# Attention with a Fourier mixing layer on one core: scores and S^T read their 512 moving columns from two halves of the tile in turn

## The chip, the cores and the metric

One core of a Trainium2 chip. The metric is the device time of one execution in microseconds. The kernel before took 2922.96 us, the median of three runs (2922.64 to 2923.09).

## The reference

Two independent branches, whose outputs stand side by side in the last dimension. S is 2048, D is 1024, all in float32.

```python
# branch A: attention with 32 heads of 32 columns
qkv = (x @ wqkv).reshape(B, S, 3, H, Dh) -> q, k, v per head
scores = einsum("bhqd,bhkd->bhqk", q, k) * Dh ** -0.5
p = softmax(scores, axis=-1)
o = einsum("bhqk,bhkd->bhqd", p, v)
a_out = o.reshape(B, S, D) @ wo
# branch B: real part of a 2-d Fourier transform with given matrices
a = einsum("bsd,ed->bse", x, dft_hid_re)
b = einsum("bsd,ed->bse", x, dft_hid_im)
b_out = einsum("ts,bse->bte", dft_seq_re, a) - einsum("ts,bse->bte", dft_seq_im, b)
```

## The kernel before

TensorE works on tiles of 128 partitions. Dense products (q, k, v, branch B, the output projection) are built from sums and differences of blocks, so that fewer products are needed, and each operand is split into a high and a low half, so that a product takes three matmuls in the narrower float32 form (`fp32r`). All these matmuls are issued at line 414, in groups that accumulate into one PSUM tile: `pd` (pool psD, two buffers), or `psT` where the attention doesn't use it. The text calls them dense matmuls; the code calls their list `fills`.

The attention goes head by head. For head h, `QS` (`qs`) and `KS` (`ks`) hold 96 rows of q and k (three copies of 32 rows, high and low halves, so that one matmul gives the full product), 2048 columns, and two more rows: ones in `KS`, and in `QS` first zeros and later the negated row maxima in two halves. Three streams are issued for each head:

- **S, scores** (line 1853 in `scores`). For a tile of 128 queries (the stationary operand, from `QS`, or from the copy `QX`, `qx`, for the first four) and a half of the keys, two matmuls of 512 moving columns of `KS` fill a `psS` tile of 128 x 1024. VectorE takes the row maximum (line 1859), ScalarE the exponential and its sum over the row (line 1862). Only maxima and sums are kept. There are 16 x 2 x 2 = 64 such matmuls a head.
- **T, transposed scores S^T** (line 1975 in `transposed`). For each of 16 tiles t of 128 keys (stationary, `KS`) and each of four blocks j of 512 queries (moving, `QS`), one matmul fills a `psT` tile; ScalarE writes its exponential to a `pt` tile (line 1979). 64 matmuls a head. They wait for the maxima, which get into `QS` by two small DMAs (`m_d<-lt`, `qs<-m_d`).
- **V, products with V** (line 1994). After 5, 10 and 16 of the tiles t, four products for each t, one for each j, run side by side on 32 columns of the array each (`tile_position=(0, j * DH)`), with the `pt` tile as the moving operand in plain float32. They accumulate in a `pd` tile whose partition block j holds the 32 output columns of query block j. VectorE copies the first of the three results to `ot` (line 2005) and adds the other two (line 2007). Then the row sums' reciprocals (`rt`, natural order of queries) are multiplied in (line 2023, on GpSimd or VectorE) and `ot` is stored.

The order on every engine is made at build time by a small planner (class `Plan`), which steps through a model with a cost for each operation: `MM` for one dense, S or T matmul, `PV` for the four products of one t, `EVAC` for an evacuation. In the loop at the end of the kernel it picks the next work of TensorE: streams S, T and V by their readiness and a lead that S may have, and dense matmuls where none is ready or where the dense work has fallen behind its share: `nf / (FILL - RES) <= done / ATT`, with `ATT` the planned TensorE time of the attention. Dense matmuls that are left when the attention ends make the tail of the program.

Of the kernel before, what the change touches and what calls it, by code (L numbers as in the profile page):

```python
# [11 lines left out]
ALU = mybir.AluOpType  # L12
# [4 lines left out]
P = 128  # L17
S = 2048
D = 1024
H = 32  # L20
# [3 lines left out]
NB = 512  # L24
# [198 lines left out]
def kernel(  # L223
# [12 lines left out]
    nc = tc.nc  # L236
# [115 lines left out]
    ORDER = (1, 2, 5, 6, 7, 3, 4)  # L352
    OUTERS = [(0, q) for q in (1, 5, 6, 7, 3, 2, 4)] + [(1, q) for q in ORDER]
    TWO = {(1, q) for q in ORDER} | {(0, 2), (0, 4)}
    MM, PV, SWITCH, TINY = 0.2275, 0.853, 0.40, 0.17
    ES, ET = 1.235, 0.625
    MAX, EVAC, CAST, BIT = 1.22, 0.685, 0.415, 0.275
    SUB = 1.31
# [11 lines left out]
    SFIRST = 0.6  # L370
    ADD = 0.68
    FILL = 3 * (7 * 24 * 4 + sum(7 * 2 * 4 if (r, q) in TWO else 8 * 8 for r in range(2) for q in ORDER) + 7 * 8 * 8 +  7 * 8 * 3)
    ATT = H * (128 * MM + 16 * PV + 3 * SWITCH)


    zeros, ps = pre.tile([P, NB], F32, name="c", tag="c", bufs=3), psD.tile([P, NB], F32, name="pd")
# [5 lines left out]
    op = pl.op  # L382
# [184 lines left out]
        return Piece(xh, xl, mx, mine), Piece(wh, wl, mw, wmine)  # L567

    whole = lambda t: t

    def chunk(p, c):
        return p, lambda t: t[:, c, :]
# [35 lines left out]
    att_gate = []  # L608
# [1212 lines left out]
    got = {}  # L1821
# [7 lines left out]
    def scores(h):  # L1829
        ST = {}  # L1830
        sold, suse = small["st"].take()
        maxes, exps = [], []
        if h:
            xold, xuse = qx_r.take()

            def load_x():
                att()
                g, r0 = divmod(h, 4)
                nc.sync.dma_start(f(QX[0])[0 : 3 * DH], qk_d[2 * g][0][r0 * DH : r0 * DH + DH].rearrange("d i c -> (d i) c"))

            got[h, "x"] = op("SP", ISSUE, load_x, [*xold, *qk_st[2 * (h // 4)][0], *(att_gate if h == 1 else [])], [xuse], -2, 192)
        for n, (qt, c) in enumerate([(k % 4, k // 4) for k in range(8)] + [divmod(k, 2) for k in range(8, 32)]):
            old, users = psS_r.take()
            own = h > 0 and qt < 4
            box = {}

            def mm(n=n, qt=qt, c=c, box=box, own=own):
                if n == 0:
                    ST["negm"] = sm.tile([P, 2, NS], F32, name="negm", bufs=2)
                    ST["sums"] = sm.tile([P, 2, NS], F32, name="sums", bufs=2)  # L1850
                box["p"] = p = psS.tile([P, 1024], F32, name="psS")
                for i in range(2):
                    nc.tensor.matmul(  # L1853
                        p[:, i * NB : i * NB + NB], (QX[0] if own else QS[h % 2])[:, qt * P : qt * P + P],
                        KS[h % 2][:, c * 1024 + i * NB : c * 1024 + i * NB + NB], start=True, stop=True,
                    )

            def mx(qt=qt, c=c, box=box):
                nc.vector.tensor_reduce(out=ST["negm"][:, c, qt : qt + 1], in_=box["p"], axis=AX.X, op=ALU.max, negate=True)  # L1859

            def ex(qt=qt, c=c, box=box):
                nc.scalar.activation(box["p"], box["p"], AF.Exp, bias=ST["negm"][:, c, qt : qt + 1], accum_out=ST["sums"][:, c, qt : qt + 1])  # L1862

            a = op("PE", 2 * MM, mm, [*old, *([got.get((h, "x"))] if own else [got.get((h, 0, qt // 4)), got.get((h, "z"))]), got.get((h, 1, 2 * c)), got.get((h, 1, 2 * c + 1))],
                   [users, xuse] if own else [users])
            b = op("DVE", MAX, mx, [a] + (sold if n == 0 else []), [users, suse], 0)
            e = op("ACT", ES, ex, [b], [users, suse], 0)
            exp_of[a] = e
            maxes.append(b)
            exps.append(e)  # L1870
            Sops.setdefault(h, []).append(a)
            streams["S"].append((a, h, n))
            if n == 5 and h:
                sums(h - 1)

        nold, nuse = small["nm"].take()
        lold, luse = small["lh"].take()
        box = {}

        def nmin():  # L1880
            ST["nm"] = sm.tile([P, NS], F32, name="nm", bufs=2)
            nc.vector.tensor_reduce(out=ST["nm"], in_=ST["negm"].rearrange("p c n -> p n c"), axis=AX.X, op=ALU.min)

        def high():
            box["l"] = sm.tile([P, 2, NS], F32R, name="lh", bufs=2)
            nc.vector.tensor_reduce(out=box["l"][:, 0], in_=ST["negm"].rearrange("p c n -> p n c"), axis=AX.X, op=ALU.min)

        def low():
            nc.vector.tensor_tensor(out=box["l"][:, 1], in0=ST["nm"], in1=f(box["l"])[:, 0], op=ALU.subtract)
# [12 lines left out]
        mine[h] = (ST, suse, nuse, exps, moved)  # L1902
# [59 lines left out]
    def transposed(h):  # L1962
        moved = mine[h][4]
        todo = []
        po = {}
        oold, ouse = ot_r.take()
        for t in range(NS):
            for j in range(4):
                old, users = psT_r.take()
                pold, puse = pt_r.take()  # L1970
                box = {}

                def mm(t=t, j=j, box=box):
                    box["p"] = psT.tile([P, NB], F32, name="psT")
                    nc.tensor.matmul(box["p"], KS[h % 2][:, t * P : t * P + P], QS[h % 2][:, j * NB : j * NB + NB], start=True, stop=True)  # L1975

                def ex(box=box):
                    box["t"] = att_low().tile([P, NB], F32, name="pt", bufs=NPT)
                    nc.scalar.activation(box["t"], box["p"], AF.Exp)  # L1979

                a = op("PE", MM, mm, [*old, *moved, *(att_gate if h == t == j == 0 else []), *(got.get((h, w, k)) for w, k in ((0, j), (1, t // 4)))], [users])
                e = op("ACT", ET, ex, [a, *pold], [users, puse], -1, 0, pt_r)
                exp_of[a] = e
                streams["T"].append((a, h, 4 * t + j))
                Tops.setdefault(h, []).append(a)
                todo.append((t, j, box, e, puse))
            if t + 1 in ENDS:
# [14 lines left out]
                def gather_o(t0=t0):  # L2002
                    if t0 == 0:
                        po["o"] = att_low().tile([P, NB], F32, name="ot", bufs=2)
                        nc.vector.tensor_copy(po["o"], po["p"])
                    else:
                        nc.vector.tensor_tensor(out=po["o"], in0=po["o"], in1=po["p"], op=ALU.add)

                e = op("DVE", EVAC, gather_o, [v] + (oold if t0 == 0 else []), [ouse], -1)
                streams["V"].append((v, h, e))  # L2010
# [155 lines left out]
```

## Time and profile before

| | before |
|---|---|
| median of three runs | 2922.96 us |
| profiled execution, its own time | 2929.45 us |
| its span | 2927.7 us |
| mean granted clock of TensorE | 0.999 |
| matmul records: dense, line 414 | 6528 |
| scores, line 1853 | 2048 |
| S^T, line 1975 | 2048 |
| products with V, line 1994 (two for each) | 4096 |

The profile is one execution of the program. Its page gives the busy time of each engine and groups of instructions by line; a matmul's span reaches from its start to the end of its drain, so spans of consecutive matmuls overlap, and the time that one takes up is read from the distance between starts in the timeline. "PEld" are the weight loads, which run beside the matmuls. In a group, the numbers after the bar are the busy time in us, the mean span of one in ns, and the idle time of the engine ahead of them with what ended most of it.

### The profile page before, as it was taken

The numbers are of one execution on the slowest core, as the hardware profiler recorded it, in microseconds if no ns is written. First come the engines' busy times: TensorE is split into PE (matmuls) and PEld (weight loads), VectorE is DVE, ScalarE is ACT, GpSimd is POOL, SyncE is SP. The second block draws the span as 40 slices with busy tenths as digits, with TensorE's granted clock in tenths as the row PEclk, the third lists the DMA queues.
The fourth block names the chain that finished last, engine by engine and source line by source line (L and its number), as shares of the span: only waits on it lengthen the run. The fifth ranks groups of instructions, "written<-read, shape, count | busy, mean of one in ns | idle before, by whom it ended". The sixth has DMA issues, their size and how long they took to land.

```text
span 2927.7 us, 47039 instructions
## 1 busy us (share of the span) xinstructions
PE 2904.0 (99%) x14728; PEld 2107.2 (72%) x14728; DVE 2386.5 (82%) x3251; ACT 2373.3 (81%) x4509; POOL 1241.3 (42%) x975
## 2 busy tenths in 40 slices
PE   9999999999999999999999999999999999999999
PEld 8887776777667777777676677667667777777777
DVE  7679888788788887788888898888988788788745
ACT  5348898888888888988999898898889888888741
POOL 2325534142233433337655456666675352243200
PEclk9999999999999999999999999999999999999999
DMA  9989978697789988867899776887876665677558
GB/s 345 349 298 328 314 225 272 222 346 269 268 289 339 309 297 287 291 213 218 291 348 333 226 223 216 276 272 229 271 229 208 204 180 181 193 246 226 188 191 287
DMA packets 485844, 768.18 MB, mean 262 GB/s; under 512 B 120382, under 2 KB 153406, under 8 KB 485470
## 3 DMA queue, kind: packets, MB, share of 16 engines
q1 hardware_dynamic: 485452, 765.04, 79.4%
q8 instruction: 119, 1.95, 0.3%
q14 instruction: 129, 1.06, 0.1%
q10 hardware_dynamic: 144, 0.13, 0.0%
HBM read 511.74 MB, written 253.25 MB: 261 GB/s over the span
## 4 chain that ended last, share of the span: by engine, by line
PE 75%; DMA 4%; DVE 1%; ACT 1%; SPq 0%; issue 0%; POOL 0%; DVEq 0%; ACTq 0%; POOLq 0%
PE pd L414 34%; PE psT L1975 14%; PE pd L1994 13%; PE psS L1853 13%; PE psT L414 2%; ACT psS L1862 1%; DVE negm L1859 1%; DMA qs<-m_d 1%; DMA slot<-in_ct 0%; DMA g<-in_ct 0%; DMA hl<-ha_d 0%; ACT pt L1979 0%; DMA m_d<-lt 0%; DMA ha_d<-slot 0%; DMA g<-g_d 0%
## 5 line engine op out<-in xcount | busy, mean ns | idle before, releaser
L414 PE MATMUL pd<-slot,hl 128*128 128x512 f32 x5028 | 1446.7, 390 | 4.2 <-DMA hl<-ha_d 1.4
L1979 ACT ACTIVATE pt<-psT 128x512 f32<-128x512 f32 x2048 | 1191.5, 668 | 260.7 <-PE psT L1975 258.5
L1859 DVE TENSOR_REDUCE negm<-psS 128x1 f32<-128x1024 f32 x1024 | 1240.7, 1221 | 198.3 <-PE psS L1853 190.1
L1862 ACT ACTIVATE psS<-psS,negm 128x1024 f32<-128x1024 f32 x1024 | 1189.2, 1161 | 47.4 <-DVE negm L1859 44.5
L414 PEld LDWEIGHTS pd<-slot,hl 128*128 128x128 f32 x5028 | 943.6, 188 | 204.8 <-DVE negm L1859 2.7
L1975 PE MATMUL psT<-qs,ks 128*128 128x512 f32 x2048 | 802.4, 395 | 4.4 <-DMA qs<-m_d 3.2
L1975 PEld LDWEIGHTS psT<-qs,ks 128*128 128x128 f32 x2048 | 382.2, 188 | 160.0 <-issue 53.0
L1853 PE MATMUL psS<-ks,qs 128*128 128x512 f32 x1552 | 473.1, 391 | 4.2 <-ACT psS L1862 4.2
L1994 PE MATMUL pd<-pt,vt 128*32 128x512 f32 x4096 | 460.9, 596 | 1.2 <-DVE e L723 0.9
L1853 PEld LDWEIGHTS psS<-ks,qs 128*128 128x128 f32 x1552 | 289.5, 188 | 69.1 <-ACT psS L1862 11.0
L504 POOL TENSOR_TENSOR slot<-raw,slot 128x512 fp32r<-128x512 f32 x153 | 196.2, 1291 | 316.1 <-DVE slot L501 116.6
L1994 PEld LDWEIGHTS pd<-pt,vt 128*32 128x32 f32 x4096 | 123.4, 110 | 285.1 <-issue 268.3
L504 POOL TENSOR_TENSOR slot<-slot,slot 128x512 fp32r<-128x512 f32 x183 | 234.3, 1292 | 206.1 <-DVE slot L501 54.5
L1862 ACT ACTIVATION_READ_ACCUMULATOR psS<-psS,negm 128x1 f32 x1024 | 287.0, 280 | 0.0
L504 POOL TENSOR_TENSOR hl<-raw,hl 128x512 fp32r<-128x512 f32 x122 | 156.8, 1289 | 257.4 <-DVE hl L501 84.7
L479 POOL TENSOR_TENSOR raw<-raw,g 128x512 f32<-128x512 f32 x119 | 153.3, 1291 | 226.6 <-ACT pt L1979 31.3
L414 PE MATMUL pd<-slot,slot 128*128 128x512 f32 x780 | 210.6, 389 | 0.1
L414 PEld LDWEIGHTS pd<-slot,slot 128*128 128x128 f32 x780 | 146.4, 188 | 30.9 <-DVE e L723 0.4
L1853 PE MATMUL psS<-ks,qx 128*128 128x512 f32 x496 | 151.0, 394 | 3.3 <-ACT psS L1862 3.2
L479 DVE TENSOR_TENSOR raw<-raw,g 128x512 f32<-128x512 f32 x141 | 103.3, 738 | 23.6 <-DMA g<-in_ct 6.6
L1853 PEld LDWEIGHTS psS<-ks,qx 128*128 128x128 f32 x496 | 91.7, 188 | 34.6 <-issue 9.2
L479 POOL TENSOR_TENSOR slot<-slot,slot 128x512 f32<-128x512 f32 x79 | 102.1, 1302 | 27.5 <-DVE slot L479 11.3
(140 smaller groups left out, 2167.6 us busy)
## 6 DMA issues: line engine op xcount, KB each, us to landing
hl<-ha_d SPq DMA_DIRECT2D x134, 512.0 KB
slot<-in_ct SPq DMA_DIRECT2D x144, 256.0 KB
qk_d<-e SPq DMA_DIRECT2D x52, 512.0 KB
qs<-qk_d SPq DMA_DIRECT2D x128, 192.0 KB
ks<-qk_d SPq DMA_DIRECT2D x128, 192.0 KB
raw<-g_d SPq DMA_DIRECT2D x96, 256.0 KB
ha_d<-hl SPq DMA_DIRECT2D x42, 512.0 KB
raw<-in_ct SPq DMA_DIRECT2D x80, 256.0 KB
```

What stands on the lines that cost most here:

```text
L414: nc.tensor.matmul(box["ps"], a[1]((a[0].hi, a[0].lo)[u]()), b[1]((b[0].hi, b[0].lo)[v]()), start=k == 0, stop=k == n - 1)
L479: (nc.gpsimd if e == "POOL" else nc.vector).tensor_tensor(out=dest(), in0=dest() if a is None else a.get(), in1=other["q"] if "q" in other ...
L504: (nc.gpsimd if e == "POOL" else nc.vector).tensor_tensor(out=lo(), in0=raw(), in1=f(hi()), op=ALU.subtract)
L1853: nc.tensor.matmul(p[:, i * NB : i * NB + NB], (QX[0] if own else QS[h % 2])[:, qt * P : qt * P + P], KS[h % 2][:, c * 1024 + i * NB : c * ...
L1859: nc.vector.tensor_reduce(out=ST["negm"][:, c, qt : qt + 1], in_=box["p"], axis=AX.X, op=ALU.max, negate=True)
L1862: nc.scalar.activation(box["p"], box["p"], AF.Exp, bias=ST["negm"][:, c, qt : qt + 1], accum_out=ST["sums"][:, c, qt : qt + 1])
L1975: nc.tensor.matmul(box["p"], KS[h % 2][:, t * P : t * P + P], QS[h % 2][:, j * NB : j * NB + NB], start=True, stop=True)
L1979: nc.scalar.activation(box["t"], box["p"], AF.Exp)
L1994: nc.tensor.matmul(po["p"][j * DH : j * DH + DH, :], VT[h][:, k, :], box["t"], start=(k == t0), stop=(k == t), tile_position=(0, j * DH),)
```

## The change

The moving operand of each S and T matmul is read through a view that takes its 512 columns in the order 0, 256, 1, 257, and so on. In S this permutes the keys within a tile, and maxima and sums over keys don't depend on their order. In T it permutes the queries within a block of 512, so the `pt` tile and the result of the products with V have their queries in the new order; the copy and the additions that take this result out of PSUM read it with a step of two and write the two halves of `ot` one after the other, which restores the order. The planner gets a cost `MS` for these matmuls.

```diff
-    MM, PV, SWITCH, TINY = 0.2275, 0.853, 0.40, 0.17
+    MM, MS, PV, SWITCH, TINY = 0.2275, 0.2165, 0.853, 0.40, 0.17
...
-    ATT = H * (128 * MM + 16 * PV + 3 * SWITCH)
+    ATT = H * (128 * MS + 16 * PV + 3 * SWITCH)
...
+    def turns(t):
+        return t.rearrange("p (i n) -> p n i", i=2)
+    def order_of(t):
+        return t.rearrange("p (n i) -> p i n", i=2)
+    def as_two(t):
+        return t.rearrange("p (i n) -> p i n", i=2)
...
                     nc.tensor.matmul(
                         p[:, i * NB : i * NB + NB], (QX[0] if own else QS[h % 2])[:, qt * P : qt * P + P],
-                        KS[h % 2][:, c * 1024 + i * NB : c * 1024 + i * NB + NB], start=True, stop=True,
+                        turns(KS[h % 2][:, c * 1024 + i * NB : c * 1024 + i * NB + NB]), start=True, stop=True,
...
-            a = op("PE", 2 * MM, mm, [*old, ...
+            a = op("PE", 2 * MS, mm, [*old, ...
...
-                    nc.tensor.matmul(box["p"], KS[h % 2][:, t * P : t * P + P], QS[h % 2][:, j * NB : j * NB + NB], start=True, stop=True)
+                    nc.tensor.matmul(box["p"], KS[h % 2][:, t * P : t * P + P], turns(QS[h % 2][:, j * NB : j * NB + NB]), start=True, stop=True)
...
-                a = op("PE", MM, mm, [*old, *moved, ...
+                a = op("PE", MS, mm, [*old, *moved, ...
...
-                        nc.vector.tensor_copy(po["o"], po["p"])
+                        nc.vector.tensor_copy(as_two(po["o"]), order_of(po["p"]))
                     else:
-                        nc.vector.tensor_tensor(out=po["o"], in0=po["o"], in1=po["p"], op=ALU.add)
+                        nc.vector.tensor_tensor(out=as_two(po["o"]), in0=as_two(po["o"]), in1=order_of(po["p"]), op=ALU.add)
```

The lines move down by 11: scores are issued at line 1864, S^T at 1986, the products with V at 2005, and their evacuations at 2016 and 2018. Since the planner works with the new cost, the order moves too. On TensorE, in the middle of the attention (after the last products with V of the sixth head), the rhythm of before is this, with dense matmuls (line 414) between S^T and scores:

```order
L1994 MATMUL pd<-pt,vt 32x512 x24
L1975 MATMUL psT<-qs_709,ks_710 128x512 x2
L1853 MATMUL psS<-ks_2716,qx 128x512 x4
L414 MATMUL pd<-slot_5667,hl 128x512
L1975 MATMUL psT<-qs_709,ks_710 128x512
L414 MATMUL pd<-slot_6181,hl 128x512
L1975 MATMUL psT<-qs_709,ks_710 128x512
L414 MATMUL pd<-slot_6181,hl 128x512 x2
L414 MATMUL pd<-slot_6208,hl 128x512 x3
```

And at the same place of the changed kernel:

```order
L2005 MATMUL pd<-pt,vt 32x512 x24
L1986 MATMUL psT<-qs_709,ks_710 128x512 x2
L1864 MATMUL psS<-ks_2717,qx 128x512 x4
L414 MATMUL pd<-slot_4928,hl 128x512
L1986 MATMUL psT<-qs_709,ks_710 128x512
L414 MATMUL pd<-slot_4928,hl 128x512
L1986 MATMUL psT<-qs_709,ks_710 128x512
L414 MATMUL pd<-slot_4928,hl 128x512
L414 MATMUL pd<-slot_4968,hl 128x512 x3
```

The rhythm of the streams is the same; the dense matmuls between them are others, from another point of their list. On TensorE at the end of the attention, around the last products with V of the program, before:

```order
L1975 MATMUL psT<-qs_2715,ks_2716 128x512
L414 MATMUL pd<-slot_31285,hl 128x512 x2
L414 MATMUL pd<-slot_31291,hl 128x512 x3
L414 MATMUL pd<-slot_31306,hl 128x512 x3
L1994 MATMUL pd<-pt,vt 32x512 x24
L414 MATMUL pd<-slot_31314,hl 128x512 x3
L414 MATMUL psT<-slot_30483,hl 128x512 x3
```

And changed:

```order
L1986 MATMUL psT<-qs_2716,ks_2717 128x512
L414 MATMUL pd<-slot_30654,hl 128x512
L414 MATMUL pd<-slot_30915,hl 128x512 x3
L414 MATMUL pd<-slot_31189,hl 128x512 x3
L2005 MATMUL pd<-pt,vt 32x512 x24
L414 MATMUL pd<-slot_31194,hl 128x512 x3
L414 MATMUL pd<-slot_31221,hl 128x512 x3
```

From the last products with V to the end, 153 rows of dense matmuls stood before (459 matmuls) and 139 stand now (417): 42 matmuls have moved from the tail into the attention.

More of the change, by code (lines that the diff above doesn't have):

```diff
@@ L1862, in ex @@
                 nc.scalar.activation(box["p"], box["p"], AF.Exp, bias=ST["negm"][:, c, qt : qt + 1], accum_out=ST["sums"][:, c, qt : qt + 1])
-            a = op("PE", 2 * MM, mm, [*old, *([got.get((h, "x"))] if own else [got.get((h, 0, qt // 4)), got.get((h, "z"))]), got.get((h, 1, 2 * c)), got.get((h, 1, 2 * c + 1))],
+            a = op("PE", 2 * MS, mm, [*old, *([got.get((h, "x"))] if own else [got.get((h, 0, qt // 4)), got.get((h, "z"))]), got.get((h, 1, 2 * c)), got.get((h, 1, 2 * c + 1))],
                    [users, xuse] if own else [users])
@@ L1979, in ex @@
                     nc.scalar.activation(box["t"], box["p"], AF.Exp)
-                a = op("PE", MM, mm, [*old, *moved, *(att_gate if h == t == j == 0 else []), *(got.get((h, w, k)) for w, k in ((0, j), (1, t // 4)))], [users])
+                a = op("PE", MS, mm, [*old, *moved, *(att_gate if h == t == j == 0 else []), *(got.get((h, w, k)) for w, k in ((0, j), (1, t // 4)))], [users])
                 e = op("ACT", ET, ex, [a, *pold], [users, puse], -1, 0, pt_r)
```

## The prediction

> **What bounds the kernel now.** I read the head of the page first: the span, the busy time of each engine, and by slice the clock that TensorE was granted.
>
> ```profile
> span 2927.7 us, 47039 instructions
> PE 2904.0 (99%) x14728; PEld 2107.2 (72%) x14728; DVE 2386.5 (82%) x3251; ACT 2373.3 (81%) x4509; POOL 1241.3 (42%) x975
> PEclk9999999999999999999999999999999999999999
> ```
>
> TensorE (PE) has only 2927.7 - 2904.0 = 23.7 us of the span without a matmul under way, at full clock all along, and no other engine is busy for more than 82%. The second view is the list of waits, cut to TensorE:
>
> ```profile
> PE psS L1853 <- ACT psS L1862: 7.4, 9, 1.9
> PE psT L1975 <- DMA qs<-m_d: 3.2, 4, 1.7
> ...
> PE psT L1975 <- ACT pt L1979: 1.1, 2, 0.6
> ```
>
> Its longest entry is 7.4 us in nine waits. So the time is the sum of what TensorE streams, and a matmul that gets shorter or longer moves the end almost undiluted. Third come the groups of the page: how many matmuls of each kind there are, and what ScalarE (ACT) and VectorE (DVE) spend on the tiles that these fill.
>
> ```profile
> L1979 ACT ACTIVATE pt<-psT 128x512 f32<-128x512 f32 x2048 | 1191.5, 668 | 260.7 <-PE psT L1975 258.5
> L1859 DVE TENSOR_REDUCE negm<-psS 128x1 f32<-128x1024 f32 x1024 | 1240.7, 1221 | 198.3 <-PE psS L1853 190.1
> ...
> L1975 PE MATMUL psT<-qs,ks 128*128 128x512 f32 x2048 | 802.4, 395 | 4.4 <-DMA qs<-m_d 3.2
> L1975 PEld LDWEIGHTS psT<-qs,ks 128*128 128x128 f32 x2048 | 382.2, 188 | 160.0 <-issue 53.0
> L1853 PE MATMUL psS<-ks,qs 128*128 128x512 f32 x1552 | 473.1, 391 | 4.2 <-ACT psS L1862 4.2
> L1994 PE MATMUL pd<-pt,vt 128*32 128x512 f32 x4096 | 460.9, 596 | 1.2 <-DVE e L723 0.9
> ...
> L1853 PE MATMUL psS<-ks,qx 128*128 128x512 f32 x496 | 151.0, 394 | 3.3 <-ACT psS L1862 3.2
> ```
>
> The change touches 2048 + 1552 + 496 = 4096 matmuls. Their mean of 391 to 395 ns isn't what one costs, since each begins before the last one has drained. The cost is the step from start to start, which the timeline shows where no wait falls between (columns: start, us, engine, line, tile, shape, count). First one row of products with V, then a stretch of all kinds:
>
> ```profile
> 655.30 5.36 PE L1994 MATMUL pd<-pt,vt 128*32 128x512 f32 x48 [0.22 <-DVE c L671]
> ```
>
> ```profile
> 700.53 0.61 PE L1853 MATMUL psS<-ks,qs 128*128 128x512 f32 x2
> 700.98 0.39 PE L1975 MATMUL psT<-qs,ks 128*128 128x512 f32 x1
> 701.21 0.39 PE L414 MATMUL pd<-slot,hl 128*128 128x512 f32 x1
> 701.43 0.39 PE L1975 MATMUL psT<-qs,ks 128*128 128x512 f32 x1
> 701.66 1.07 PE L414 MATMUL pd<-slot,hl 128*128 128x512 f32 x4
> 702.57 0.61 PE L1853 MATMUL psS<-ks,qs 128*128 128x512 f32 x2
> ...
> 705.38 4.50 PE L1994 MATMUL pd<-pt,vt 128*32 128x512 f32 x40
> ```
>
> From 700.53 to 702.57 nine matmuls start, scores, S^T and dense ones alike: 2.04/9 = 0.2267 us each. The products with V give the measure to set beside this, here with the first and last start of all their records:
>
> ```profile
> L1994 PE MATMUL pd<-pt,vt x4096: 592/592/1061, 278.0 to 2818.0; 128*32 128x512 f32 x196
> ```
>
> Eight more of these records (48 against 40) take 5.36 - 4.50 = 0.86 us. Their outputs are 32 partitions wide, so four run side by side, each reading its own tile, and a set of four takes 0.43 us. A product leaves two records, and such a set takes nearly twice the 0.2267 us of the other matmuls; I read this as two passes over the columns in each record, 0.43/2 = 0.215 us for 512 columns. On this reading the array and PSUM can take 512 columns in 0.215 us, and a matmul that reads one run of 512 words takes 11.7 ns longer.
>
> By the Trainium skill, "TensorE: Matmul & The Clock Gate", section "Wait — 56ns, not 53.3ns?", warm matmuls of 512 columns start 215.7 ns apart. The trace agrees for the products with V and not for the matmuls of 226.7 ns; that figure as the new step would make the saving 45.1 us in place of the 47.9 below.
>
> **The change part by part.** *The moving operand in turns.* 4096 matmuls read column 0 of the first half, column 0 of the second, column 1 of the first, and so on. No row of before shows such a read. The bounds come from the products with V. At best reading stops being a limit and the step falls to 0.215 us (0.2125 if both times are rounded unluckily); at worst every word that isn't next to the last one needs an access of its own, and the matmul goes at the pace of a single stream there, 512 words in 0.43 us. I take 0.215. The 11.7 ns are the same for each of the tiles read (ks, qs, hl) and whatever DMA, ScalarE and VectorE do meanwhile, so they look like a limit of one run of words; and four streams from four tiles, which together read 4 x 512 words in 0.43 us, twice the words per time of the single run, don't show them. Two halves in turn are nearer to this case than to one stream at half pace, though two words from one port are not two streams; that is the weak point. Sum: 4096 x 0.0117 = 47.9 us off.
>
> *Weight loads.* Unchanged in number, 188 ns each, and they lie under the matmul before. 188 is still under 215, so they don't become the bound; what is left as cover falls from 39 to 27 ns.
>
> *Putting the queries right.* The 96 evacuations of the products with V (32 copies, 64 additions) read PSUM with a step of two words.
>
> ```profile
> L2007 DVE TENSOR_TENSOR ot<-ot,pd 128x512 f32<-128x512 f32 x64 | 43.9, 686 | 85.0 <-PE pd L1994 84.9
> ...
> L2005 DVE COPY ot<-pd 128x512 f32<-128x512 f32 x32 | 22.1, 690 | 26.3 <-PE pd L1994 26.2
> ```
>
> Bounds: as now, 0.69 us; or as if the skipped words were read too, 1024 columns, 1.22 us by the L1859 row. That is 0 to 96 x 0.53 = 51 us on VectorE over the 2540 us of the attention stage (278 to 2818). A gain is excluded since no word less is read. I cost it at nothing on the end: VectorE waits 85.0 + 26.3 us just ahead of these very instructions, and while they run TensorE has S^T, scores and the other accumulator bank to go on with. Behind them on VectorE stand row maxima, so without that cover it is the exponentials, and then scores, that come late, by at most those 51 us.
>
> *The order.* The planner reckons 0.2165 for these matmuls instead of 0.2275 and moves dense matmuls forward: after the last product with V there stand 139 rows of three matmuls, and there were 153. Those 14 x 3 = 42 matmuls (9.5 us) leave the tail and enter the attention stage; TensorE runs each of them once either way, so this adds nothing. Their DMA loads and the casts ahead of them move with them.
>
> *What gets late next.* The attention stage gets shorter with the same exponentials and maxima in it.
>
> Busy time in two windows of it (PE, weight loads, DVE, ACT, POOL, each with its count; then clock, DMA share and GB/s):
>
> ```profile
> 600.00:800.00 200.00, 199.20 (x1037) 140.25 (x1028) 165.89 (x225) 173.52 (x333) 66.13 (x52) 1.00 0.85 294
> ...
> 1400.00:1600.00 200.00, 199.17 (x1034) 138.82 (x1033) 177.84 (x241) 182.76 (x349) 116.61 (x92) 1.00 0.95 323
> ```
>
> ACT is busy in them for 87% and, at the fullest, 91%. The stage loses 47.9 - 9.5 = 38 of its 2540 us, 1.5%, so 87% becomes 88%, and 91% becomes 93%: tighter, not full. The waits of TensorE on ACT and on the maxima's DMA, 7.4 + 3.2 + 1.1 = 11.7 us, will grow; I give back 8 us, an estimate of two thirds more.
>
> *Sum.* The profiled execution took 2929.45 us with a span of 2927.7, 6.5 above the median of the runs, 2922.96. In its span: 2927.7 - 47.9 + 8 = 2887.8. Against the median: 2922.96 - 39.9 = **2883 us**.
>
> **Rivals.** *A word from elsewhere costs an access of its own* (the other side). Place: each of the 4096 matmuls, on TensorE itself, with nothing to hide it. Price at the full bound: (0.43 - 0.2267) x 4096 = 833 us, time 3756; with half the words held over, some 3340. It decides from a step of 0.2281 on, where 1.4 ns x 4096 passes the 5.8 us that are 0.2%. For it speaks that all reads of before are of words in a row, so nothing shows the opposite; against it, that four scattered streams at once run unhindered. I give it 0.18.
>
> The Trainium skill, "Advanced Engine Details and Errata", section "Memory Cachelines", stands on this rival's side: SBUF is read in lines of 16 bytes, two hits on a line are needed to cover the latency, and a new line at each access is penalised. In turn, every word is on another line than the one before. No run here shows it yet; if each line is held until its four words are used, the rule doesn't bite.
>
> *The 11.7 ns aren't of reading* but of, say, changing 128 weight columns per matmul where the products with V change 32. Then the change doesn't do what it says: the step stays 0.2267, VectorE has up to 51 us more, mostly covered, and the order is planned for a pace that isn't there: 2925. For it: the width of the weights differs too between the rows that I compare. 0.08.
>
> *The exponentials hold the pace.* Scores come sooner, but psS has two buffers and each is freed by ACT. If half of the gain is lost in these waits: 2899 to 2903. Against it stand ACT's 87% and 7.4 us. 0.06.
>
> **How the numbers follow.** The forecast has 0.68; its own range is 2864 (step 0.2125, nothing given back) to 2899. With the held pace and the unchanged step the range is 2862 to 2930, which leaves out 0.18 for the costly read. A measurement of this kernel can tell about 0.2%, 5.8 us, from no change: faster 0.68 + 0.06 = 0.74, same 0.08, slower 0.18.
>
> **What would show it.** The groups of the two changed lines should have a mean near 380 ns (391 to 395 less 11.7) and the timeline steps of 0.215 between them, with the dense matmuls still at 0.227; near 390 means the second rival, near 590 the first. The two evacuation lines show 0.69 to 1.22 us. TensorE's waits on ACT should stay under 20 us and ACT's share in the attention windows rise to 88%. I am wrong altogether if the step doesn't change, or grows, or if TensorE's idle time rises by more than some 25 us.

## The result, and the profile after

The changed kernel took 2902.96 us, the median of four runs (2897.03 to 2908.37), against 2923.03 us before: ratio 0.9931, 95% interval 0.9914 to 0.9948. It is faster by 20 us, half of the 40 that were forecast. Its runs are 11.4 us apart, those of before 1 us. The profiled execution was its fastest, 2897.03 us, while the one of before was 6.5 us above the median; so the two profiles are 32 us apart, and 12 of these are the scatter of single executions.

The head of the page of the changed kernel:

```profile
span 2894.9 us, 47047 instructions
PE 2868.7 (99%) x14728; PEld 2110.3 (73%) x14728; DVE 2364.3 (82%) x3249; ACT 2362.7 (82%) x4485; POOL 1268.1 (44%) x1001
```

TensorE is still the bound. Its groups, line by line:

```profile
L414 PE MATMUL pd<-slot,hl 128*128 128x512 f32 x5076 | 1487.2, 392 | 1.7 <-DVE hl L504 1.2
...
L1986 PE MATMUL psT<-qs,ks 128*128 128x512 f32 x2048 | 779.6, 384 | 1.2 <-DMA qs<-m_d 0.7
...
L1864 PE MATMUL psS<-ks,qs 128*128 128x512 f32 x1552 | 457.4, 380 | 9.7 <-ACT psS L1873 9.5
...
L1864 PE MATMUL psS<-ks,qx 128*128 128x512 f32 x496 | 144.9, 383 | 4.3 <-ACT psS L1873 3.9
...
L2018 DVE TENSOR_TENSOR ot<-ot,pd 128x512 f32<-128x512 f32 x64 | 44.0, 687 | 93.4 <-PE pd L2005 93.2
```

Scores and S^T fell from 391 to 395 ns to 380 to 384, as forecast. But the dense matmuls at line 414, which read as before, went from 390 to 392; their group before was this:

```profile
L414 PE MATMUL pd<-slot,hl 128*128 128x512 f32 x5028 | 1446.7, 390 | 4.2 <-DMA hl<-ha_d 1.4 <-DVE negm L1859 1.3 <-POOL hl L504 0.8
```

Two nanoseconds in a mean of thousands are worth a look, and the timeline shows where they are (start, us, engine, line, tile, shape, count):

```profile
1300.33 0.59 PE L1864 MATMUL psS<-ks,qx 128*128 128x512 f32 x2
1300.76 0.39 PE L414 MATMUL pd<-slot,hl 128*128 128x512 f32 x1
1300.99 0.38 PE L1986 MATMUL psT<-qs,ks 128*128 128x512 f32 x1
1301.20 0.39 PE L414 MATMUL pd<-slot,hl 128*128 128x512 f32 x1
1301.43 0.38 PE L1986 MATMUL psT<-qs,ks 128*128 128x512 f32 x1
1301.65 1.08 PE L414 MATMUL pd<-slot,hl 128*128 128x512 f32 x4
1302.57 0.59 PE L1864 MATMUL psS<-ks,qs 128*128 128x512 f32 x2
```

Two scores take 0.43 us, 0.215 each. A dense matmul behind one in turns takes 0.23 (1300.76 to 1300.99, and 1301.20 to 1301.43), where it took 0.2267 before. The waits of TensorE on the scores' buffers have grown too, from 7.4 us in 9 waits:

```profile
PE psS L1864 <- ACT psS L1873: 13.5, 25, 1.3
...
PE psT L1986 <- DMA qs<-m_d: 0.7, 2, 0.4
...
PE psT L1986 <- ACT pt L1990: 0.3, 1, 0.3
```

The trace holds the start of every matmul. Summing the distances from each start to the next by the kind of the first one shares out TensorE's whole time, waits included. In us, for the profiled executions of before, of the changed kernel, and of the experiments below. The second row is the kernel before as it ran behind the blocks of the last experiment, a second trace of it, which started with its first loads done; the column "all" is left out there. The last two columns are the mean step of a dense matmul directly behind scores or S^T, and of the second one behind (only steps up to 241 ns, so without waits):

| | dense | scores | S^T | V | with the warm-up, all | first behind, ns | second, ns |
|---|---|---|---|---|---|---|---|
| before | 1494.6 | 477.1 | 489.5 | 456.3 | 2921.0 | 227.2 | 226.9 |
| before, behind blocks | 1492.9 | 475.1 | 488.2 | 453.8 | | 227.2 | 227.0 |
| changed | 1505.1 | 453.6 | 473.9 | 452.7 | 2888.8 | 230.9 | 229.4 |
| changed, again | 1506.7 | 454.4 | 474.2 | 456.1 | 2895.1 | 231.0 | 229.4 |
| turns, old order | 1510.7 | 452.8 | 466.6 | 453.2 | 2887.0 | 231.0 | 228.9 |
| order alone | 1490.8 | 478.6 | 495.6 | 454.4 | 2923.0 | 227.0 | 226.8 |
| scores only, old order | 1510.9 | 450.3 | 497.3 | 452.7 | 2914.7 | 230.3 | 231.3 |
| all in turns, old order | 1437.6 | 465.0 | 501.9 | 454.0 | 2862.0 | 215.8 | 215.9 |
| all in turns, replanned | 1431.1 | 463.4 | 490.8 | 456.5 | 2845.4 | 215.9 | 215.8 |

From the first row to that of the changed kernel, scores and S^T lost 39.1 us. Their steps without waits went from 227.9 and 227.4 to 215.5 and 215.4 ns, about 50 us in 4096 matmuls; so some 11 us came back as longer waits. Dense matmuls gained 10.5 us. Against the second trace of before, which has fewer waits, scores and S^T lost 35.8 us, so that some 14 came back, and dense matmuls gained 12.2. The changed kernel's second profile gives 34.7, 15 and 13.8.

Two theories came out of this. *Neighbours and waits*: a matmul that reads words in a row runs slower behind one that reads in turns, whatever the order. *Order*: the planner's new order waits more, by itself. They may both hold, and the experiments take them apart.

### The profile page after: what moved, and what is told of

It reads as the page before. It is cut to its first block, busy times and chain, and to the rows that moved or that the text cites. A ratio compares the mean times of both kernels' runs of the same rounds, so it can differ in the third digit from the quotient of the medians.

```text
span 2894.9 us, 47047 instructions
## 1 busy us (share of the span) xinstructions
PE 2868.7 (99%) x14728; PEld 2110.3 (73%) x14728; DVE 2364.3 (82%) x3249; ACT 2362.7 (82%) x4485; POOL 1268.1 (44%) x1001
## 4 chain that ended last, share of the span: by engine, by line
PE 69%; DMA 2%; ACT 2%; DVE 1%; issue 0%; SPq 0%; POOL 0%; DVEq 0%; ACTq 0%; POOLq 0%
PE pd L414 33%; PE psT L1986 12%; PE pd L2005 12%; PE psS L1864 11%; PE psT L414 2%; ACT psS L1873 1%; ACT pt L1990 1%; DVE negm L1870 0%; DMA g<-in_ct 0%; DMA ks<-qk_d 0%; DMA qs<-m_d 0%; DMA hl<-ha_d 0%; DMA m_d<-lt 0%; DMA g<-so_d 0%; DMA o_d<-ot 0%
## 5 line engine op out<-in xcount | busy, mean ns | idle before, releaser
L414 PE MATMUL pd<-slot,hl 128*128 128x512 f32 x5076 | 1487.2, 392 | 1.7 <-DVE hl L504 1.2
L414 PEld LDWEIGHTS pd<-slot,hl 128*128 128x128 f32 x5076 | 953.9, 188 | 189.4 <-DVE hl L504 1.6
L1986 PE MATMUL psT<-qs,ks 128*128 128x512 f32 x2048 | 779.6, 384 | 1.2 <-DMA qs<-m_d 0.7
L1864 PE MATMUL psS<-ks,qs 128*128 128x512 f32 x1552 | 457.4, 380 | 9.7 <-ACT psS L1873 9.5
L479 POOL TENSOR_TENSOR raw<-raw,g 128x512 f32<-128x512 f32 x147 | 189.7, 1294 | 243.4 <-DMA raw<-in_xb 25.3
L504 POOL TENSOR_TENSOR hl<-raw,hl 128x512 fp32r<-128x512 f32 x111 | 142.5, 1287 | 209.7 <-DVE hl L501 42.5
L1864 PE MATMUL psS<-ks,qx 128*128 128x512 f32 x496 | 144.9, 383 | 4.3 <-ACT psS L1873 3.9
L2018 DVE TENSOR_TENSOR ot<-ot,pd 128x512 f32<-128x512 f32 x64 | 44.0, 687 | 93.4 <-PE pd L2005 93.2
L1343 POOL TENSOR_TENSOR slot<-slot 128x512 f32<-128x512 f32 x44 | 56.7, 1293 | 143.5 <-DMA slot<-in_ct 71.5
```

The lines of the kernel that those rows point to most:

```text
L414: nc.tensor.matmul(box["ps"], a[1]((a[0].hi, a[0].lo)[u]()), b[1]((b[0].hi, b[0].lo)[v]()), start=k == 0, stop=k == n - 1)
L479: (nc.gpsimd if e == "POOL" else nc.vector).tensor_tensor(out=dest(), in0=dest() if a is None else a.get(), in1=other["q"] if "q" in other ...
L504: (nc.gpsimd if e == "POOL" else nc.vector).tensor_tensor(out=lo(), in0=raw(), in1=f(hi()), op=ALU.subtract)
L1343: made = op("POOL", SUB, lambda e, part=part, kind=ALU.add if terms[1][0] > 0 else ALU.subtract: (nc.gpsimd if e == "POOL" else nc.vector) ...
L1864: nc.tensor.matmul(p[:, i * NB : i * NB + NB], (QX[0] if own else QS[h % 2])[:, qt * P : qt * P + P], turns(KS[h % 2][:, c * 1024 + i * NB ...
L2018: nc.vector.tensor_tensor(out=as_two(po["o"]), in0=as_two(po["o"]), in1=order_of(po["p"]), op=ALU.add)
```

## The experiments

**The order apart from the reads.** Two kernels: the turns with the planner's old number, so that every engine has the order of before; and the new order with the reads and evacuations of before.

```diff
-    MM, MS, PV, SWITCH, TINY = 0.2275, 0.2165, 0.853, 0.40, 0.17
+    MM, MS, PV, SWITCH, TINY = 0.2275, 0.2275, 0.853, 0.40, 0.17
```

> The reads in turns are kept, the planner gets 0.2275 for scores and S^T again, so that every engine has the order of before. Theory 'order': the 20 us that are missing against the forecast were lost by the new order, so the old order gives about 2883 to 2890. Theory 'neighbours and waits': dense matmuls behind a matmul in turns take 4 ns more (10 us in all) and TensorE waits more on ACT whatever the order, so the time is 2898 to 2908 again, and the step of a dense matmul behind scores or S^T is again near 0.231.

Measured: 2895.86 us (2891.96 to 2898.72), ratio 0.9903, interval 0.9887 to 0.9919. This lies between the two ranges, so neither theory has all of it.

```diff
-                        turns(KS[h % 2][:, c * 1024 + i * NB : c * 1024 + i * NB + NB]), start=True, stop=True,
+                        KS[h % 2][:, c * 1024 + i * NB : c * 1024 + i * NB + NB], start=True, stop=True,
...
-                    nc.tensor.matmul(box["p"], KS[h % 2][:, t * P : t * P + P], turns(QS[h % 2][:, j * NB : j * NB + NB]), start=True, stop=True)
+                    nc.tensor.matmul(box["p"], KS[h % 2][:, t * P : t * P + P], QS[h % 2][:, j * NB : j * NB + NB], start=True, stop=True)
...
-                        nc.vector.tensor_copy(as_two(po["o"]), order_of(po["p"]))
+                        nc.vector.tensor_copy(po["o"], po["p"])
                     else:
-                        nc.vector.tensor_tensor(out=as_two(po["o"]), in0=as_two(po["o"]), in1=order_of(po["p"]), op=ALU.add)
+                        nc.vector.tensor_tensor(out=po["o"], in0=po["o"], in1=po["p"], op=ALU.add)
```

> The changed order (planner at 0.2165) with the reads and the evacuations of before. Theory 'order': the new order is worse by itself, 2930 to 2945. Theory 'neighbours and waits': the order by itself is worth nothing, 2920 to 2927, and the dense matmuls are back at 0.2267 behind scores and S^T.

Measured: 2933.07 us (2926.87 to 2937.82), ratio 1.0031, interval 1.0020 to 1.0042. So the new order by itself costs 9 us against the 2923.72 of the kernel before, and with the old order the turns bring 28 us. The old order beats the changed kernel by about 7 us (5 us against its second set of runs below), but there the intervals overlap. The theory of neighbours holds as well: with the old order the dense step behind a matmul in turns is 231.0 ns, and with the new order and no turns it is 227.0. What the new order costs is seen in the table's sums for scores and S^T, 478.6 + 495.6 us against 477.1 + 489.5. Most of it stands between an S^T and the scores that follow: the steps over 241 ns there exceed the usual 227 by 17.7 us in all, against 8.9 before.

TensorE's first row of waits in the kernel with the order alone, against 7.4 us in 9 waits before:

```profile
PE psS L1864 <- ACT psS L1873: 10.4, 21, 1.1
```

**The grain of the turns.** Next, reads in pairs of neighbouring words: for the dense matmuls (with PSUM written in the same order, so that nothing has to be put right), and for scores and S^T.

```diff
-nc.tensor.matmul(box["ps"], a[1]((a[0].hi, a[0].lo)[u]()), b[1]((b[0].hi, b[0].lo)[v]()), start=k == 0, stop=k == n - 1)
+nc.tensor.matmul(pairs(box["ps"]), a[1]((a[0].hi, a[0].lo)[u]()), pairs(b[1]((b[0].hi, b[0].lo)[v]())), start=k == 0, stop=k == n - 1)
...
+    def pairs(t):
+        return t.rearrange("p (i n k) -> p n i k", i=2, k=2)
```

> As the changed kernel, and the dense matmuls too read their 512 columns from two halves, in pairs of neighbouring words (0, 1, 256, 257, ...), and write PSUM in the same order of pairs, so that each column lands at its own place. Theory 'one run': any matmul that reads one run of words is held to 0.2267 and two runs lift it, so the dense step falls to 0.2155 and the extra 4 ns go too: 6528 matmuls go from 1505 to about 1420 us, and with an order planned for slower ones 2825 to 2860. Rival: pairs on the PSUM side cost what the reads gain, or more: dense step 0.227 or above, 2900 or above.

Measured: 3568.32 us, ratio 1.2203 (1.2186 to 1.2220). Neither side of the expectation had this size.

```diff
     def turns(t):
-        return t.rearrange("p (i n) -> p n i", i=2)
+        return t.rearrange("p (i n k) -> p n i k", i=2, k=2)
...
     def order_of(t):
-        return t.rearrange("p (n i) -> p i n", i=2)
+        return t.rearrange("p (n i k) -> p i n k", i=2, k=2)
...
     def as_two(t):
-        return t.rearrange("p (i n) -> p i n", i=2)
+        return t.rearrange("p (i n k) -> p i n k", i=2, k=2)
```

> As the changed kernel, with scores and S^T reading pairs of neighbouring words from the two halves in turn (0, 1, 256, 257, ...) and the evacuation put right accordingly. Theory 'one run': two runs are enough whatever the grain, step 0.2155 and 2895 to 2908. Rival 'grain': the gain comes from each word being apart from the word before it, so pairs keep part of the 11 ns: step 0.220 to 0.2267, 2912 to 2925.

Measured: 3384.26 us, ratio 1.1572 (1.1557 to 1.1588). The groups of the kernel with pairs in scores and S^T, and below them the dense group of the kernel with dense pairs:

```profile
L1986 PE MATMUL psT<-qs,ks 128*128 128x512 f32 x2048 | 1029.0, 507 | 0.0
L1864 PE MATMUL psS<-ks,qs 128*128 128x512 f32 x1552 | 642.6, 504 | 2.4 <-ACT psS L1873 2.4
```

```profile
L414 PE MATMUL pd<-slot,hl 128*128 128x512 f32 x5076 | 2020.0, 503 | 1.1 <-DVE hl L504 1.1
```

The span of a matmul went from 384 to 507 ns and its step to 0.333 us. The dense matmuls in pairs, with PSUM written in pairs as well, have the same step (median 0.333), so the writing isn't what costs. Both theories fall: two runs in turn don't relieve the read by being two.

A third grain: one run with a step of two, so that no word follows its neighbour.

```diff
     def turns(t):
-        return t.rearrange("p (i n) -> p n i", i=2)
+        return t.rearrange("p (n i) -> p i n", i=2)
...
-                        nc.vector.tensor_copy(as_two(po["o"]), order_of(po["p"]))
+                        nc.vector.tensor_copy(order_of(po["o"]), as_two(po["p"]))
                     else:
-                        nc.vector.tensor_tensor(out=as_two(po["o"]), in0=as_two(po["o"]), in1=order_of(po["p"]), op=ALU.add)
+                        nc.vector.tensor_tensor(out=order_of(po["o"]), in0=order_of(po["o"]), in1=as_two(po["p"]), op=ALU.add)
```

> As the changed kernel (its order too), but scores and S^T read their 512 columns with a step of two: 0, 2, 4, ... and then 1, 3, 5, ...; the evacuation is put right accordingly. After the runs with pairs (step 0.333) the theory of two runs doesn't hold as it stood. Theory 'neighbours in the tile': a read is held up when the word before it was its neighbour, so the step is 0.2155 here too and the time 2895 to 2908. Theory 'halves': it is the jump between two distant places word by word that helps, so a single run with a step keeps 0.2267 or more: 2925 to 2940 with this order. If lines of four words matter, only two words of each are used at a visit, and the step may be as long as with pairs, 3380.

Measured: 3865.51 us, ratio 1.3219 (1.3200 to 1.3238). That is worse than pairs:

```profile
L1986 PE MATMUL psT<-qs,ks 128*128 128x512 f32 x2048 | 1278.5, 629 | 0.0
```

The step is about 0.45 us, so it isn't distance from the neighbour that helps either.

**Only the scores in turns**, S^T and all else as before, in the old order.

```diff
-    MM, MS, PV, SWITCH, TINY = 0.2275, 0.2165, 0.853, 0.40, 0.17
+    MM, MS, PV, SWITCH, TINY = 0.2275, 0.2275, 0.853, 0.40, 0.17
...
-                    nc.tensor.matmul(box["p"], KS[h % 2][:, t * P : t * P + P], turns(QS[h % 2][:, j * NB : j * NB + NB]), start=True, stop=True)
+                    nc.tensor.matmul(box["p"], KS[h % 2][:, t * P : t * P + P], QS[h % 2][:, j * NB : j * NB + NB], start=True, stop=True)
...
-                        nc.vector.tensor_copy(as_two(po["o"]), order_of(po["p"]))
+                        nc.vector.tensor_copy(po["o"], po["p"])
                     else:
-                        nc.vector.tensor_tensor(out=as_two(po["o"]), in0=as_two(po["o"]), in1=order_of(po["p"]), op=ALU.add)
+                        nc.vector.tensor_tensor(out=po["o"], in0=po["o"], in1=po["p"], op=ALU.add)
```

> Only the scores are read in turns; S^T, the products with V and their evacuation are as before, and the order is that of before (planner 0.2275). Theory 'whoever follows': any matmul that reads words in a row and comes behind one in turns takes 4 ns more, so S^T behind scores stands at 0.231 as the dense ones did. 2048 x 11.5 ns = 23.5 us less for scores, 5 to 8 us of it back in those that follow: 2905 to 2909. Rival 'dense only': the longer step comes from the dense operands; S^T behind scores stays at 0.2267, 2901 to 2904.

Measured: 2922.71 us (2917.46 to 2926.53), ratio 0.9994, interval 0.9986 to 1.0003: nothing is left of 25 us. Its timeline shows how:

```profile
1302.06 0.59 PE L1864 MATMUL psS<-ks,qx 128*128 128x512 f32 x2
1302.49 0.39 PE L1986 MATMUL psT<-qs,ks 128*128 128x512 f32 x1
1302.72 0.39 PE L414 MATMUL pd<-slot,hl 128*128 128x512 f32 x1
1302.95 0.40 PE L1986 MATMUL psT<-qs,ks 128*128 128x512 f32 x1
1303.18 1.08 PE L414 MATMUL pd<-slot,hl 128*128 128x512 f32 x4
1304.10 0.59 PE L1864 MATMUL psS<-ks,qx 128*128 128x512 f32 x2
```

It is the nine matmuls of the rhythm that the prediction quoted, and they take 2.04 us, as they did there. The two scores take 0.43 where they took 0.45; the seven behind them, all reading in a row, take 1.61, 0.230 each. S^T is slowed like the dense ones, so it is the manner of reading and not the operand; and the time lies above both expected ranges, since the effect lasts for about six matmuls rather than one: over the whole trace the first six behind the scores take 231, 231, 235, 229, 232 and 230 ns in the mean, and from the seventh on 227.

**All in turns.** If it is the mixture that costs, then without a mixture it should go. Here the dense matmuls read in turns as well, and the evacuations of all dense products read PSUM with a step of two (`Turned` marks such an operand, and `right` gives the other operands of the instruction the shape of two halves).

```diff
-    MM, MS, PV, SWITCH, TINY = 0.2275, 0.2165, 0.853, 0.40, 0.17
+    MM, MS, PV, SWITCH, TINY = 0.2275, 0.2275, 0.853, 0.40, 0.17
...
-nc.tensor.matmul(box["ps"], a[1]((a[0].hi, a[0].lo)[u]()), b[1]((b[0].hi, b[0].lo)[v]()), start=k == 0, stop=k == n - 1)
+nc.tensor.matmul(box["ps"], a[1]((a[0].hi, a[0].lo)[u]()), turns(b[1]((b[0].hi, b[0].lo)[v]())), start=k == 0, stop=k == n - 1)
...
-        frees.append(finish(lambda: box["ps"], o))
+        frees.append(finish(lambda: Turned(box["ps"]), o))
...
-                        nc.vector.tensor_copy(A.at(), ps())
+                        right(nc.vector.tensor_copy)(A.at(), ps())
...
```

> Dense matmuls read in turns too, and each evacuation of a dense product reads PSUM with a step of two, as that of the products with V does; the order is that of before. If the longer dense step is an effect between the two kinds of reading, it is gone: all matmuls at 0.2155. From the 2895.9 of the run with the old order, dense 6528 x 0.231 = 1511 us become 6528 x 0.2155 + 13 of longer waits = 1420: 2805, and some 15 to 30 of it lost to ScalarE and VectorE, which then are busy 85% of the span: 2805 to 2840. Rival 'dense operands are of another kind': the step stays above 0.2267 and the time is 2895 or more.

Measured: 2864.40 us (2860.61 to 2871.85), ratio 0.9796, interval 0.9780 to 0.9812. The same with the planner at 0.2165 for every matmul:

```diff
-    MM, MS, PV, SWITCH, TINY = 0.2275, 0.2165, 0.853, 0.40, 0.17
+    MM, MS, PV, SWITCH, TINY = 0.2165, 0.2165, 0.853, 0.40, 0.17
```

> As the run with everything in turns, but the planner reckons 0.2165 for every matmul, dense ones too. Theory 'costs must be true': the order of the changed kernel was worse by 8 us because the planner had dense matmuls at 0.2275 beside 0.2165, while they took 0.231; with true costs its order is no worse than the old one: 2795 to 2835. Rival 'the order is luck': one order is as good as another within 10 us either way, whatever the costs: up to 10 us above the run with the old order.

Measured: 2857.32 us (2854.09 to 2860.64), ratio 0.9772, interval 0.9759 to 0.9785. Each beats the kernel before and the changed one; the second is 46 us below the changed kernel. The groups of the replanned one:

```profile
L446 PE MATMUL pd<-slot,hl 128*128 128x512 f32 x5160 | 1440.6, 380 | 7.3 <-POOL hl L536 2.9 <-ACT hl L531 1.8 <-POOL slot L536 1.2
```

```profile
L404 DVE TENSOR_TENSOR e<-slot,pd 128x512 f32<-128x512 f32 x155 | 105.7, 682 | 29.8 <-PE pd L446 26.4 <-DMA raw<-g_d 2.2
```

Dense matmuls are at 380 ns, their step behind any neighbour at 215.8, and the evacuations that read PSUM with a step of two (line 404) take 682 ns where those in a row took 682 to 683; the largest group of them before:

```profile
L1091 DVE TENSOR_TENSOR e<-slot,pd 128x512 f32<-128x512 f32 x72 | 49.1, 682 | 10.8 <-PE pd L414 8.8 <-issue 0.5
```

Both kernels fell short of the expectation, 2805 to 2840 and 2795 to 2835. Where that went is in the table: by their steps alone 2048 matmuls take 442 us, but scores take 463.4 and S^T 490.8, against 453.6 and 473.9 in the changed kernel. With shorter matmuls the waits on ScalarE come more often. In the replanned kernel these are TensorE's waits for a scores buffer:

```profile
PE psS L1886 <- ACT psS L1895: 19.8, 34, 2.2
```

With the old order it is the weight loads of S^T that wait for a `psT` buffer, until ScalarE has written the exponential. The three rows are of the old order, of the replanned kernel and of the kernel before:

```profile
PEld psT L2008 <- ACT pt L2012: 133.1, 704, 1.0
```

```profile
PEld psT L2008 <- ACT pt L2012: 17.2, 61, 1.5
```

```profile
PEld psT L1975 <- ACT pt L1979: 9.5, 35, 1.0
```

The granted clock has a part in it too: its mean is 0.997 in both of these profiles and 0.999 in that of before, and 0.002 of 2860 us are some 6 us, as an estimate.

The two expectations on the order can't be told apart by the times: replanning brought 7 us here, with intervals that overlap, although it took away most of the waits of the weight loads.

**The changed kernel again, and with a truer cost for the dense matmuls.**

> The changed kernel once more, unaltered, on the chip of the next two. Its four runs were 11.4 us apart, and its profiled one was the fastest of them. If that is the kernel's own spread, the time lies at 2897 to 2908 again with a ratio of 0.9931 within 0.002, and the granted clock of a profile with a longer span is below 1.0 for some 3.4 us windows; if the first set was odd, the median moves by more than 5 us.

Measured: 2900.93 us (2898.80 to 2902.74), ratio 0.9922, interval 0.9909 to 0.9936. The first result stands, at its lower side.

```diff
-    MM, MS, PV, SWITCH, TINY = 0.2275, 0.2165, 0.853, 0.40, 0.17
+    MM, MS, PV, SWITCH, TINY = 0.2305, 0.2165, 0.853, 0.40, 0.17
```

> The changed kernel with the planner told what its dense matmuls really take beside reads in turns: 0.2305 in place of 0.2275, and 0.2165 for scores and S^T as it has. Theory 'costs must be true': the 8 us that the new order lost come back, 2890 to 2897. Rival 'the order is luck': no gain, 2897 to 2910, since a longer dense step in the plan doesn't touch the places where TensorE waits for the exponentials.

Measured: 2896.08 us (2893.80 to 2901.81), ratio 0.9910, interval 0.9896 to 0.9925. That is 5 us less, within the range of the first theory, but the intervals overlap, so it is not settled whether true costs or luck with the order make these few microseconds.

**The step by itself.** Blocks of 48 matmuls on a tile of zeros ahead of the kernel's work.

```diff
+    z = zeros.bitcast(F32R)
+    for k in range(48):
+        nc.tensor.matmul(ps, z[:, 0:P], z, start=True, stop=True)
...
+    for k in range(48):
+        nc.tensor.matmul(ps, z[:, 0:P], z.rearrange("p (a i n) -> p a n i", i=2, n=4), start=True, stop=True)
```

> The kernel before with blocks of 48 matmuls ahead of its work, on a tile of zeros, each block with another order of its 512 moving columns or another number of weight columns: in a row with 128, 64 and 32 weight columns; two halves in turn with 128 and 32; pairs in turn with 128 and 32; evens first with 128 and 32; quarters in turn; two runs in turn at distances of 128, 64, 32, 16, 8, 4 and 2 words; fours in turn; and last, in turns and in a row by turns. It is slower by the blocks, some 250 us, and only the steps count. Theory 'moving read alone': the step depends on the order of the moving columns and not on the weights: in a row 0.2267 with 32 weight columns too, pairs 0.333 and evens 0.45 with 32 too. Rival 'weights beside it': the moving read loses time to the load of the next weights, so with 32 weight columns a row falls to 0.215 or 0.217, and pairs and evens fall with it. In the mixed block, behind one in turns, a row takes 0.231.

Its timeline; the blocks come in the order of the text above, and the step of a block is the distance to the next row's start over 48:

```profile
4.74 11.04 PE L382 MATMUL pd<-c 128*128 128x512 f32 x48
15.62 11.20 PE L384 MATMUL pd<-c 128*64 128x512 f32 x48
26.65 11.28 PE L386 MATMUL pd<-c 128*32 128x512 f32 x48
37.77 10.52 PE L388 MATMUL pd<-c 128*128 128x512 f32 x48
48.13 10.52 PE L390 MATMUL pd<-c 128*32 128x512 f32 x48
58.49 16.16 PE L392 MATMUL pd<-c 128*128 128x512 f32 x48
74.48 16.41 PE L394 MATMUL pd<-c 128*32 128x512 f32 x48
90.73 21.93 PE L396 MATMUL pd<-c 128*128 128x512 f32 x48
112.48 21.94 PE L398 MATMUL pd<-c 128*32 128x512 f32 x48
134.24 13.77 PE L400 MATMUL pd<-c 128*128 128x512 f32 x48
147.84 10.52 PE L402 MATMUL pd<-c 128*128 128x512 f32 x48
...
199.64 10.52 PE L412 MATMUL pd<-c 128*128 128x512 f32 x48
210.00 11.04 PE L414 MATMUL pd<-c 128*128 128x512 f32 x48
220.88 12.17 PE L416 MATMUL pd<-c 128*128 128x512 f32 x48
232.89 0.38 PE L418 MATMUL pd<-c 128*128 128x512 f32 x1
233.11 0.39 PE L419 MATMUL pd<-c 128*128 128x512 f32 x1
```

| order of the 512 columns | step, us, 128 weight columns | 32 |
|---|---|---|
| in a row | 0.2267 | 0.2317 |
| two halves in turn (256 words apart) | 0.2158 | 0.2158 |
| two runs in turn, 128, 64, 32, 16, 8 or 4 words apart | 0.2158 | |
| two runs in turn, 2 words apart | 0.2267 | |
| fours of neighbours, from two halves in turn | 0.2502 | |
| four quarters in turn | 0.2833 | |
| pairs of neighbours, from two halves in turn | 0.333 | 0.339 |
| evens first | 0.453 | 0.453 |

The order of the moving read sets the step. Fewer weight columns make a row no faster: it takes 0.2298 with 64 and 0.2317 with 32. The steps are those of the kernel on a tile that nothing else touches, and most blocks ran while no DMA and no other engine was at work, as the window from 134 to 210 us shows (PE, weight loads, DVE, ACT, POOL, clock, DMA share, GB/s):

```profile
134.00:210.00 76.00, 76.00 (x337) 63.62 (x336) 0.00 (x0) 0.00 (x0) 0.00 (x0) 1.00 0.00 1
```

In the mixed block one in turns takes 0.215 and one in a row 0.231 in the mean, as expected.

## Why the prediction was right in direction and twice too large

- **What bounds it: right.** TensorE is busy 98% or more in all of these kernels, and what its steps lost went into the time.
- **The step of scores and S^T: right in value, with a reason that fell.** 0.215 was taken, 0.2155 measured; 47.9 us was the term, about 50 the steps without waits. But it was argued that two runs in turn are near to four streams from four tiles. Four quarters in turn take 0.2833, so more runs don't relieve the read. As far as that reason goes, the value was hit by luck: 0.215 is the time that the products with V had shown, no order that was tried goes below it, and no run says why two halves in turn reach it.
- **"The dense matmuls still at 0.227": wrong.** This is the step that failed first. They were taken to be independent of what runs before them. Behind a matmul in turns they take 0.231, then 0.229, which came to 10.5 us in the profile, and to 12 and 14 in the two profiles of the changed kernel beside the second trace of before. The sum had nothing for this. The scores-only kernel shows the cause, and the kernels with everything in turns show it gone.
- **"The order ... adds nothing": wrong.** Only the 42 moved matmuls were counted. The new order alone costs 9 us (1.0031), in waits of TensorE. The give-back of 8 us for waits was near the truth for what it was meant for: with the old order, scores and S^T lost 43.9 us of their 50 beside the second trace of before (452.8 + 466.6 against 475.1 + 488.2), so 6 came back. With the new order 14 to 15 came back. So the saving is 50 us of steps, less 14 or 15 of longer waits, less 12 to 14 in the dense matmuls: 21 to 24, beside the 20 that were measured. Single executions scatter by more than the rest.
- **Weight loads: right.** Those of scores and S^T still take 188 ns (median), and the step of 0.2155 holds beside them.
- **Putting the queries right: right.** Copies take 692 ns and additions 688 (medians), where they took 691 and 687.
- **ACT's share: right in one window of two.** 88% from 600 to 800 us, as worked out, but 91% from 1400 to 1600 us, where 93% was forecast:

```profile
600.00:800.00 200.00, 197.02 (x1025) 144.97 (x1024) 169.33 (x231) 176.83 (x339) 64.58 (x51) 1.00 0.88 299
...
1400.00:1600.00 200.00, 195.22 (x999) 139.19 (x999) 173.45 (x235) 182.32 (x351) 120.87 (x96) 1.00 0.96 337
```

- **The rivals.** The costly read is real, only not for this order: at pairs and evens the loss is 460 and 941 us, and the worst bound of 0.43 us was even passed, at 0.453. By the page cited for it, "Advanced Engine Details and Errata" of the Trainium skill, section "Memory Cachelines", two hits on a 16-byte line cover the latency and a new line at each access is penalised. The runs say otherwise for this operand: in turns each word lies on another line than the last and nothing is lost; pairs and evens hit a line twice in succession and lose 0.106 and 0.226 us. That the 11.7 ns belong to the weights is refuted by the block with 32 weight columns. The time that the rival of the exponentials gave, 2899 to 2903, is the one that was measured, but not by its cause alone: of the 20 us that are missing, the waits hold 6 or 7 beyond the 8 given back, and 12 to 14 are in the dense matmuls. TensorE's waits on ACT, 13.5 + 0.3 us, stayed under the 20 that were set as a sign.

What stays open: why these orders rank as they do, and why reading in a row is held up for several matmuls after reads in turns (six in the scores-only kernel; in the changed kernel the third dense one takes 228 ns and the fourth 227). The steps were measured; no run looks inside the read.

## What to carry to other kernels

An access order that a trace doesn't contain costs a block of 48 matmuls to measure, and should be measured with its neighbours: the gain of one kind of matmul can be a loss of the next kind, and scores alone gave nothing where everything together gave 2.3%. When a planner's number changes, its order changes as well, and that deserves a run of its own with the old code. And a group that the change doesn't touch is worth reading first: the 2 ns on line 414 held 12 to 14 of the 20 us that were missing.

## What the runs showed of the hardware that wasn't expected

For these matmuls of 512 four-byte columns, the order of the moving words alone moves the step between 0.2158 and 0.453 us. Two runs in turn word by word are the best of the orders tried, 0.2158 at each of the seven distances from 4 to 256 words; at 2 words they are no better than a row.

TensorE's clock also drops for windows of 3.4 us, one or two in a row, after stretches in which it starves. In the profile of before (PE busy, weight loads, DVE, ACT, POOL, granted clock, DMA share, GB/s), and the row of products with V that ran in that window:

```profile
491.20:494.60 3.40, 1.86 (x6) 0.78 (x5) 2.66 (x4) 3.01 (x5) 0.39 (x1) 0.99 0.76 226
494.60:497.90 3.30, 3.14 (x16) 0.79 (x20) 2.07 (x4) 1.97 (x4) 1.27 (x1) 0.50 0.91 304
```

```profile
494.76 6.92 PE L1994 MATMUL pd<-pt,vt 128*32 128x512 f32 x48 [0.90 <-DVE e L723]
```

TensorE was busy for 1.86 of 3.4 us and then ran at half clock; the 48 records took 6.92 us, where such a row took 5.36 elsewhere, so the window cost about 1.6 us. In all the traces each such window within the work comes right behind 3.4 us in which TensorE was busy for 0.9 to 2.2 us, but not every such stretch is followed by one. The changed kernel's four runs had mean clocks of 1.000, 0.999, 0.998 and 0.998 at 2897.0, 2901.6, 2904.3 and 2908.4 us; 0.002 of the clock is 5.8 us, so these windows, with the waits that set them off, go with the spread of its runs. That they cause it wasn't tried.
